# Scalars by a product with ones, masks behind the branch, and GpSimd set-up behind the first sink columns: the head of a fused attention and mixture-of-experts kernel

## The chip, the cores and the metric

The kernel runs on one core of one Trainium2 chip. The metric is the device time of one execution in microseconds. All times below that carry a place ("at 7.77") are counted from the start of the profiled span.

The engines are named as in the profile: PE is TensorE (PEld its weight loads), DVE is VectorE, ACT is ScalarE, POOL is GpSimd, SP is SyncE. A q behind a name is that engine's instruction queue, which issues DMAs and takes branches.

## The reference

Three layers follow each other. The first is attention over 4 batches, 8 heads, 768 positions and 64 columns, with a causal window and a few sink positions that every query sees:

```python
keep = is_sink | in_window          # pos < n_sink, 0 <= i - j < window
scores = np.where(keep, scale * q @ k.T, -1e9)
a = softmax(scores)                 # divided by sum + 1e-9
x = (a @ v) as [3072, 512]
x = np.maximum(x @ w_in, 0) ** 2 @ w_out          # 512 -> 2048 -> 512
```

The last layer is a mixture of eight experts. Each token takes the expert with the largest logit, and its result is scaled by the softmax weight of that expert and a sigmoid gate:

```python
out[mask] = gate_w * eom * (np.maximum(x[mask] @ w1[e], 0) @ w2[e])
```

`n_sink` (4) and `window` (128) are inputs, so the kernel reads them at run time.

## The kernel before

The kernel treats the 3072 tokens in 12 blocks of 256. For each block t, attention is done in four pairs of heads (p = 0 to 3) and two halves of 128 queries (n), then the block goes through the first feed-forward layer while the attention of the next block lies between its matrix products. The last part runs the experts over tokens that were sorted by expert.

The head is the time before the feed-forward layer of block 0 begins. It holds the constants, the attention of block 0, the start of block 1, and the first of the 32 pieces (512 KB each) of w_in and w_out, which must be rebuilt from raw bits: ScalarE does L310 and L313 on a piece, VectorE L317 and L318, and only then is its staging buffer free. The staging buffers (tag "stage") are a ring of three, handed out in the order in which the program asks for them; the ring also serves the scratch of `setup` and of `setup2`. The first three pieces have buffers of their own (`braw`) and are loaded from ScalarE's queue; all later ones come from SP's queue.

The steps of the head are events with places from -46 to 0 in a list. At each place h the program emits the events due, at -38 also `setup2`, and every third place one piece of the weights. A scheduler then orders the instructions of each engine by when it expects them to be ready and by priority, with events of the head ahead of others; what is wrapped in `pin` keeps its order among the pinned ones. Each engine works through its own list in order. So what the program says late may stand early in an engine's list, if it is ready, and one instruction that waits holds all behind it.

`scalars` loads n_sink and window into one partition (`one`, from SP and ScalarE), from which VectorE works out `gen`, the flag for a general path that is not taken here, and into all partitions (`raw`, two GpSimd loads with a stride of zero), which VectorE casts to `rawf` at L124. `setup` makes the identity and the masks: GpSimd fills `rel` and `col` with positions, and VectorE compares them with the scalars and writes M0, M1 and M2 (L214 to L219). Then a dozen idle products (`fill`, L101) keep TensorE working, and every engine loads `gen` and branches (L846, L847).

Behind the branch, for each pair of heads: `prep_k` transposes k on TensorE (L373), VectorE copies it into kT (L378), and GpSimd adds four columns per key block for the sinks (L380 to L384). `prep_q` does the same for q (L404, copy L411 or L409). `scores` multiplies (L461), VectorE adds the mask and finds the extremum (L469), ScalarE takes the exponential (L472), VectorE or ScalarE normalizes (L474 to L484). `ptrans` transposes P (L501, copied by ScalarE at L505), `pv` multiplies with v (L535). `prep_sink` readies the sink rows of v: GpSimd at L435 and L436, TensorE at L438. `setup2` makes all constants that later parts need, mostly on GpSimd; it zeroes the two `psk` tiles with VectorE casts (L263) from a zeroed scratch (L250), starts two stores, and loads the gate weights from SP, on which GpSimd then works (L258 to L261).

The first feed-forward products of block 0 are at L616 and read the rebuilt pieces with even numbers; those at L641 read the odd ones.

Of the kernel before, what the change touches and what calls it, by code (L numbers as in the profile page):

```python
# [46 lines left out]
def kern(ctx, tc, q, k, v, n_sink, window, w_in, w_out, w_gate, w_og, w1, w2, out):  # L47
# [49 lines left out]
    def fill(o, n):  # L97

        w = o.shape[-1]
        for _ in range(n):  # L100
            PE.matmul(o[:, 0:w // 128 * 128], lhsT=idle[:], rhs=idle[:, None, :].broadcast_to([128, w // 128, 128]), start=True, stop=True)  # L101


    def scalars(w):

        raw = w.tile([128, 2, 2], I32, name="raw")
        one = w.tile([1, 2, 2], I32, name="one")
        SY.dma_start(out=one[:, 0], in_=n_sink.bitcast(I32)[None, :])
        A.dma_start(out=one[:, 1], in_=window.bitcast(I32)[None, :])
        G.dma_start(out=raw[:, 0], in_=n_sink.bitcast(I32)[None, :].broadcast_to([128, 2]))  # L110
        G.dma_start(out=raw[:, 1], in_=window.bitcast(I32)[None, :].broadcast_to([128, 2]))
        c = w.tile([1, 3, 4], F32, name="c")
        for n, x in ((0, 0.0), (2, 1.0)):
            V.memset(c[:, 0, n:n + 1], x)
        for n, x in ((0, float(NS)), (2, 128.0)):
            V.memset(c[:, 1, n:n + 1], x)
        for n in range(2):
            V.memset(c[:, n, 1:4:2], 0.0)
        f = one[:].rearrange("p a w -> p (a w)")
        V.tensor_tensor(out=c[:, 2], in0=f, in1=c[:, 0], op=ALU.is_lt)  # L120
        V.tensor_tensor(out=c[:, 1], in0=f, in1=c[:, 1], op=ALU.is_gt)
        V.tensor_reduce(out=c[:, 0, 0:1], in_=c[:, 1:3], axis=AX.XY, op=ALU.max)
        V.tensor_copy(out=gen[:], in_=c[:, 0, 0:1])
        V.tensor_copy(out=rawf[:], in_=raw[:])  # L124
# [77 lines left out]
    def setup():  # L202
        make_identity(nc, ident)
        tmp = [cv.tile([128, 2 * XW], F32, tag="stage", bufs=3, name="tmp")]
        ns, wd = rawf[:, 0, 0:1], rawf[:, 1, 0:1]
        rel, col = tmp[0][:, 0:260], tmp[0][:, 260:388]
# [7 lines left out]
        V.tensor_scalar(out=M2[:], in0=rel, scalar1=wd, scalar2=NEG, op0=ALU.is_ge, op1=ALU.mult)  # L214
        V.tensor_scalar(out=col, in0=col, scalar1=ns, scalar2=NEG, op0=ALU.is_ge, op1=ALU.mult)
        V.tensor_tensor(out=M0[:], in0=M2[:, 132:260], in1=col, op=ALU.max)
        V.tensor_tensor(out=M1[:, 0:128], in0=M2[:, 0:128], in1=col, op=ALU.max)
        V.tensor_copy(out=M1[:, 128:260], in_=M2[:, 128:260])
        V.tensor_copy(out=M2[:, 128:132], in_=col[:, 0:NS])  # L219
        zz = tmp[0][:, 388:389]  # L220
        V.memset(zz, 0.0)
        A.activation(out=zz, in_=zz, func=AF.Exp)

    pin = tc.keep_in_program_order

    def setup2():

        G.memset(sel[:], 0.0)
# [4 lines left out]
        G.memset(blkm[:], 1.0)  # L233
        G.affine_select(out=blkm[:], in_=blkm[:], pattern=[[-16, 8]], compare_op=ALU.is_ge, fill=0.0, base=0, channel_multiplier=1)
        G.affine_select(out=blkm[:], in_=blkm[:], pattern=[[16, 8]], compare_op=ALU.is_ge, fill=0.0, base=15, channel_multiplier=-1)
        G.memset(ones[:], 1.0)
        G.affine_select(out=tri[:], in_=ones[:], pattern=[[1, 128]], compare_op=ALU.is_gt, fill=0.0, base=0, channel_multiplier=-1)
        G.iota(ek[:], [[-1, NE]], base=NE, channel_multiplier=0, allow_small_or_imprecise_dtypes=True)
        G.iota(eb[:], [[REG, NE]], base=0, channel_multiplier=0, allow_small_or_imprecise_dtypes=True)
        G.iota(tok[:], [[128, NT // 128]], base=0, channel_multiplier=1)  # L240
        G.memset(cum[:], 0.0)
        G.iota(sio[:], [[1, 32]], base=0, channel_multiplier=0, allow_small_or_imprecise_dtypes=True)
        G.memset(ltri[:], 1.0)
# [3 lines left out]
        G.memset(pf, NT)  # L247
        SY.dma_start(out=perm[:].rearrange("(p n) o -> p (n o)", p=128), in_=pf)
        zr = tmp[:, XW:2 * XW]
        G.memset(zr, 0.0)  # L250
# [5 lines left out]
        G.memset(w3[:], 0.0)  # L256
# [109 lines left out]
    def prep_k(t, p):  # L366
# [9 lines left out]
        if t < T32:  # L376
# [6 lines left out]
            for n in range(o, 2):  # L383
                G.tensor_copy(out=kf[:, n, 128:KS], in_=sk32[:, p])  # L384
# [487 lines left out]
    for h in range(-46, 0):  # L872
        run_to(h)
        if h == -38:
            setup2()
# [315 lines left out]
```

## Time and profile before

| what | value |
|---|---|
| three runs | 1149.51, 1151.32, 1152.0 us |
| median | 1151.32 us |
| profiled execution | 1149.8 us |
| its span, from the first to the last instruction | 1148.1 us |
| TensorE busy in it | 1120.3 us (98%) |
| VectorE, ScalarE, GpSimd busy | 727.9, 637.6, 417.0 us |
| mean granted TensorE clock | 0.995 |
| instructions | 23733 |

The profiled execution is one run that the hardware profiler recorded, and its span is 1.7 us shorter than its time. A busy TensorE is not TensorE at its peak, because products overlap and their ends are modelled. In the timelines, the bracket at the end of a row gives the idle time of the engine before it and what ended that idle time.

### The profile page before, as it was taken

How to read it: one execution, taken by the hardware profiler on the slowest of the kernel's cores; microseconds unless marked ns; L12 is line 12 of the kernel's file. 1: busy time of each engine (PE TensorE's matmuls, PEld its weight loads, DVE VectorE, ACT ScalarE, POOL GpSimd, SP SyncE). 2: the span in 40 equal slices, each digit the busy share in tenths (PEclk: the TensorE clock that was granted, in tenths of full speed). 3: DMA queues.
4: the chain of work that ended last, by engine and by line, in shares of the span. 5: the costliest groups of instructions: out<-in, count | busy, mean ns of one | idle time of the engine just before them, and what ended most of it. 6: DMA issues, size and time to landing. Idle time of an engine off the chain costs nothing. (4 is left out here: it accounts for less than half of the span.)

```text
span 1148.1 us, 23733 instructions
## 1 busy us (share of the span) xinstructions
PE 1120.3 (98%) x7002; PEld 941.3 (82%) x7002; DVE 727.9 (63%) x2027; ACT 637.6 (56%) x1749; POOL 417.0 (36%) x917
## 2 busy tenths in 40 slices
PE   7999999999999999999999999999999999999995
PEld 4556788888888888888888888997788888888884
DVE  4899877576766666676667676557412576764153
ACT  4898766777676767676767767454232232232200
POOL 3112563256564336565325655310211112221111
PEclk9999999999999999999999999999999999999998
DMA  6687111121211111211112110296411456653110
GB/s 154 179 234 211 39 24 46 39 54 34 54 29 50 38 45 38 56 28 44 36 38 56 38 31 1 28 253 162 129 39 47 155 185 218 220 206 134 48 45 24
DMA packets 139392, 100.08 MB, mean 87 GB/s; under 512 B 103908, under 2 KB 112228, under 8 KB 139239
## 3 DMA queue, kind: packets, MB, share of 16 engines
q1 hardware_dynamic: 131476, 82.28, 25.8%
q0 software_dynamic: 5472, 14.19, 3.7%
q10 hardware_dynamic: 2290, 1.84, 0.5%
q8 instruction: 64, 1.05, 0.4%
q14 instruction: 90, 0.73, 0.3%
HBM read 85.56 MB, written 13.76 MB: 87 GB/s over the span
## 5 line engine op out<-in xcount | busy, mean ns | idle before, releaser
L619 PE MATMUL psh<-xT,WI 128*128 128x256 f32 x2112 | 284.8, 285 | 0.0
L619 PEld LDWEIGHTS psh<-xT,WI 128*128 128x128 f32 x2112 | 270.6, 190 | 9.7 <-issue 0.4
L956 PE MATMUL psh<-WI,xt 128*128 (+1 forms) x672 | 162.1, 395 | 1.0 <-ACT xt L936 0.7
L629 DVE TENSOR_TENSOR r<-r 128x256 f32<-128x256 f32 x180 | 82.3, 458 | 116.8 <-ACT r L622 116.7
L644 PE MATMUL psx<-WOb,h 128*128 128x512 f32 x576 | 154.0, 404 | 0.8 <-ACT h L631 0.5
L956 PEld LDWEIGHTS psh<-WI,xt 128*128 128x128 f32 x672 | 123.8, 188 | 26.8 <-ACT xt L936 1.4
L644 PE MATMUL psx<-WOa,h 128*128 128x512 f32 x528 | 143.4, 406 | 0.0
L644 PEld LDWEIGHTS psx<-WOb,h 128*128 128x128 f32 x576 | 101.8, 188 | 19.9 <-ACT h L631 1.4
L472 ACT ACTIVATE P<-P,st 128x260 f32<-128x260 f32 (+1 forms) x192 | 93.8, 489 | 42.8 <-DVE st L469 42.7
L972 DVE TENSOR_TENSOR ht<-psht,ht 128x512 fp32r<-128x512 f32 x56 | 38.5, 689 | 120.7 <-ACT ht L936 120.3
L622 ACT ACTIVATE r<-psh 128x256 f32<-128x256 f32 x192 | 71.5, 372 | 66.1 <-PE psh L619 62.9
L644 PEld LDWEIGHTS psx<-WOa,h 128*128 128x128 f32 x528 | 92.7, 189 | 15.3
L517 POOL TENSOR_SCALAR_AFFINE_SELECT PT<-PT 128x256 fp32r<-128x256 f32 x224 | 98.4, 472 | 16.2 <-DVE PT L513 16.0
L994 POOL DMA_INDIRECT out_dram<-xg,pidx x28 | 28.7, 1024 | 198.8 <-ACT xg L993 158.0
L632 DVE TENSOR_TENSOR h<-r,h 128x256 fp32r<-128x256 f32 x184 | 83.8, 456 | 17.8 <-ACT h L631 12.0
L631 ACT ACTIVATE h<-r 128x256 fp32r<-128x256 f32 x184 | 76.1, 413 | 28.8 <-DVE r L629 24.4
L469 DVE CUSTOM_DVE_ANT_0 P<-pss,M 128x260 f32<-128x260 f32 (+1 forms) x184 | 72.7, 403 | 23.1 <-PE pss L465 11.3
L985 PE MATMUL psy<-WOb,ht 128*128 (+1 forms) x336 | 84.0, 398 | 0.0
L962 ACT ACTIVATE r<-psh 128x512 f32<-128x512 f32 x48 | 28.7, 598 | 98.6 <-PE psh L956 96.8
L985 PE MATMUL psy<-WOa,ht 128*128 (+1 forms) x336 | 82.2, 392 | 0.0
L484 ACT ACTIVATE P<-P,st 128x132 f32<-128x132 f32 (+2 forms) x168 | 62.2, 415 | 35.6 <-DVE st L475 35.4
L553 POOL TENSOR_TENSOR xr<-tB,tC 128x128 f32<-128x128 f32 x80 | 38.2, 478 | 103.1 <-DVE tB L552 98.3
(450 smaller groups left out, 1958.3 us busy)
## 6 DMA issues: line engine op xcount, KB each, us to landing
raw<-in_moe_w_dram SPq DMA_DIRECT2D x36, 1024.0 KB, 5.7
craw<-in_moe_w_out_dram SPq DMA_DIRECT2D x15, 512.0 KB, 4.0
craw<-in_moe_w_in_dram SPq DMA_DIRECT2D x14, 512.0 KB, 4.1
x2tab<-x2s SPq DMA_DIRECT2D x24, 256.5 KB, 3.1
kn<-in_k_dram SPq DMA_DIRECT2D x64, 96.0 KB, 2.2
vn<-in_v_dram SPq DMA_DIRECT2D x64, 96.0 KB, 2.2
qn<-in_q_dram SPq DMA_DIRECT2D x92, 64.0 KB, 2.1
kn<-in_k_dram SPq DMA_DIRECT2D x32, 64.0 KB, 2.0
```

Source lines behind the costliest of these rows:

```text
L469: V.tensor_tensor_reduce(out=P[:, e, 0:W], in0=ps[e][:, 0:W], in1=mask[:, 0:W], scale=-SCALE, scalar=3.0e38, op0=ALU.add, op1=ALU.min, acc ...
L472: A.activation(out=P[:, e, 0:W], in_=P[:, e, 0:W], func=AF.Exp, scale=-1.0, bias=st[:, e:e + 1], accum_out=st[:, 4 + e:5 + e])
L484: A.activation(out=P[:, e, 0:W], in_=P[:, e, 0:W], func=AF.Copy, scale=st[:, 6 + e:7 + e])
L517: G.affine_select(out=both[:, 1 - b, e], in_=bf[:, 0, e], pattern=[[0, 2], [1 - 2 * b, 128]], compare_op=ALU.is_gt if b else ALU.is_ge, fi ...
L619: PE.matmul(ps[:], lhsT=WI[:, j, a_, kk, :], rhs=x[:, b_, kk, :], start=(n == 0), stop=(n == 11))
L622: A.activation(out=hq[:], in_=ps[:], func=AF.Relu)
L629: E_.tensor_tensor(out=hq[:], in0=hq[:], in1=hq[:], op=ALU.mult)
L631: A.activation(out=o[:, 0], in_=hq[:], func=AF.Copy)
L632: V.tensor_tensor(out=o[:, 1], in0=hq[:], in1=o[:, 0].bitcast(F32), op=ALU.subtract)
L644: PE.matmul(acc[t][m][:], lhsT=o[:, a_, 128 * m:128 * m + 128], rhs=WO[j // 8][:, j % 8, b_, :], start=(j == 0 and n == 0), stop=(j == NF ...
L956: PE.matmul(ps[:], lhsT=o[:, a_, kk, :], rhs=wview(n, par + 2048 * b_ + 512 * kk, 512), start=(c == 0), stop=(c == 11))
L985: PE.matmul(yp[s][:], lhsT=o[:, a_, kk, :], rhs=wview(2 + n, par + 2048 * b_ + 512 * kk, 512), start=(n == 0 and kk == 0 and c == 0), stop ...
```

## The change

`scalars` no longer loads the scalars into all partitions. It copies the one row that it has into a row of a zeroed tile, and TensorE multiplies it with a tile of ones: every partition of the result holds the scalars, and VectorE casts it from PSUM into `rawf`. Three idle products of 256 columns stand ahead of that product, and six of 512 columns behind it in place of twelve. The scratch of `setup` is now requested in `scalars`.

`setup` keeps the GpSimd part of the masks. The VectorE part is the new function `masks`; its first half (M0, and M2 as it is) stands right behind the branch, its second half (M1, and the sink columns of M2) at place -42 of the list.

`setup2` moves from place -38 to -24. Its GpSimd instructions without an operand, and the first instruction of `prep_sink(0)`, are put behind the last sink column copy of pair 1 of block 0 on GpSimd by an ordering without a semaphore (`behind`).

```diff
-    def fill(o, n):
+    def fill(o, n, keep=False):
...
-        raw = w.tile([128, 2, 2], I32, name="raw")
         one = w.tile([1, 2, 2], I32, name="one")
         SY.dma_start(out=one[:, 0], in_=n_sink.bitcast(I32)[None, :])
         A.dma_start(out=one[:, 1], in_=window.bitcast(I32)[None, :])
-        G.dma_start(out=raw[:, 0], in_=n_sink.bitcast(I32)[None, :].broadcast_to([128, 2]))
-        G.dma_start(out=raw[:, 1], in_=window.bitcast(I32)[None, :].broadcast_to([128, 2]))
...
+        wide = w.tile([128, 2 * XW], F32, tag="stage", bufs=3, name="tmp")
+        full, row = wide[:, 512:640], wide[:, 640:644]
+        V.memset(full, 1.0)
+        V.memset(row, 0.0)
+        pb = psS.tile([128, 260], F32, tag="s1", name="psb")
+        fill(pb[:, 0:256], 3, True)
+        pin(V.tensor_copy(out=row[0:1], in_=f))
+        pin(PE.matmul(pb[:, 0:4], lhsT=full, rhs=row, start=True, stop=True))
         V.tensor_tensor(out=c[:, 2], in0=f, in1=c[:, 0], op=ALU.is_lt)
...
-        V.tensor_copy(out=rawf[:], in_=raw[:])
+        pin(V.tensor_copy(out=rawf[:].rearrange("p a w -> p (a w)"), in_=pb[:, 0:4]))
+        return wide
...
+    def masks(wide, n):
+
+        rel, col = wide[:, 0:260], wide[:, 260:388]
+        ns, wd = rawf[:, 0, 0:1], rawf[:, 1, 0:1]
+        if n == 0:
+            pin(V.tensor_scalar(out=M2[:], in0=rel, scalar1=wd, scalar2=NEG, op0=ALU.is_ge, op1=ALU.mult))
+            pin(V.tensor_scalar(out=col, in0=col, scalar1=ns, scalar2=NEG, op0=ALU.is_ge, op1=ALU.mult))
+            pin(V.tensor_tensor(out=M0[:], in0=M2[:, 132:260], in1=col, op=ALU.max))
+            return
+        pin(V.tensor_tensor(out=M1[:, 0:128], in0=M2[:, 0:128], in1=col, op=ALU.max))
+        pin(V.tensor_copy(out=M1[:, 128:260], in_=M2[:, 128:260]))
+        V.tensor_copy(out=M2[:, 128:132], in_=col[:, 0:NS])
...
     def setup2():
 
-        G.memset(sel[:], 0.0)
+        behind(G.memset(sel[:], 0.0))
...
+    skd = []
+
+    def behind(x):
+
+        tc.add_manual_dep(x.ins, skd[0].ins.name, mybir.DependencyInfo(mybir.DependencyClass.NoSync, mybir.DependencyReason.DATA),
+                          reason="order")
+        return x
...
             for n in range(o, 2):
-                G.tensor_copy(out=kf[:, n, 128:KS], in_=sk32[:, p])
+                x_ = G.tensor_copy(out=kf[:, n, 128:KS], in_=sk32[:, p])
+            if t == 0 and p == 1:
+                skd.append(x_)
...
-        G.tensor_copy(out=hl[0:32], in_=t[:])
+        x_ = G.tensor_copy(out=hl[0:32], in_=t[:])
+        if b == 0:
+            behind(x_)
...
-    scalars(cv)
+    wide = scalars(cv)
     for n in range(2):
         loads(0, n, "kq")
-    setup()
+    setup(wide)
     loads(0, 0, "v")
-    fill(psT.tile([128, 512], F32, tag="T", name="psi")[:], 12)
+    fill(psT.tile([128, 512], F32, tag="T", name="psi")[:], 6, True)
...
+    masks(wide, 0)
     loads(0, 1, "v")
...
-        if h == -38:
+        if h == -42:
+            masks(wide, 1)
+        if h == -24:
             setup2()
```

## Rows read from the trace of the kernel before

**Rows 1.** The page: the profiled execution's span.
```profile
span 1148.1 us, 23733 instructions
```

**Rows 2.** Busy time by stretch: stretch, PE, PEld, DVE, ACT, POOL, granted clock, DMA share, GB/s.
```profile
5.00:10.00 5.00, 2.50 (x17) 1.40 (x15) 1.85 (x8) 0.00 (x0) 1.20 (x7) 1.00 0.45 94
10.00:15.00 5.00, 1.78 (x10) 0.88 (x11) 2.12 (x11) 0.94 (x5) 4.05 (x23) 0.93 0.89 265
...
14.00:16.00 2.00, 2.00 (x9) 0.88 (x8) 1.32 (x7) 1.49 (x8) 0.19 (x2) 0.57 0.83 188
16.00:18.00 2.00, 2.00 (x13) 1.39 (x10) 0.72 (x4) 1.43 (x6) 0.00 (x0) 0.58 0.41 92
...
44.00:1148.00 1104.00, 1085.08 (x6802) 921.53 (x6802) 702.79 (x1917) 610.72 (x1669) 404.32 (x852) 1.00 0.30 84
```

**Rows 3.** Waits, 0 to 45: us in total, times, longest.
```profile
PE psx L461 <- POOL kT L384: 2.7, 1, 2.7
```

**Rows 4.** Timeline of DVE: start, us, engine, line, operation, tiles, count [idle before].
```profile
2.29 0.15 DVE L120 TENSOR_TENSOR c<-one,c 1x4 f32<-1x4 int32 x1 [1.12 <-DMA one<-in_n_sink_dram]
...
6.16 0.17 DVE L124 CAST rawf<-raw 128x4 f32<-128x4 int32 x1 [3.29 <-DMA raw<-in_window_dram]
...
7.81 0.35 DVE L214 TENSOR_SCALAR M<-tmp,rawf 128x260 f32<-128x260 f32 x1 [1.08 <-DVEq L847]
...
8.75 0.42 DVE L378 COPY kT<-psk__624 128x256 f32<-128x256 f32 x1
...
10.05 0.42 DVE L411 COPY qT<-psq 128x256 f32<-128x256 f32 x1 [0.81 <-PE psk__705 L373]
12.65 0.42 DVE L263 CAST psk<-tmp 128x128 fp32r<-128x128 f32 x2 [2.18 <-POOL tmp L250]
...
13.32 0.28 DVE L469 CUSTOM_DVE_ANT_0 P<-pss,M 128x128 f32<-128x128 f32 x1
...
39.67 0.69 DVE L318 SCALAR_TENSOR_TENSOR fw<-craw,fw 128x512 int32<-128x512 int32 x1
...
43.26 0.69 DVE L318 SCALAR_TENSOR_TENSOR fw<-craw,fw 128x512 int32<-128x512 int32 x1
```

**Rows 5.** Timeline of PE.
```profile
1.14 4.17 PE L101 MATMUL psi<-idle 128*128 128x512 bf16 x12 [1.14 <-DVE idle L95]
...
7.77 0.39 PE L101 MATMUL psk__624<-idle 128*128 128x512 bf16 x1 [2.13 <-DVEq L847]
...
41.04 0.33 PE L373 MATMUL psk__1106<-ident,kn 128*128 128x128 f32 x1 [0.87 <-ACT PT L505]
```

**Rows 6.** Timeline of ACT and its queue.
```profile
9.47 0.38 ACTq L298 DMA_DIRECT2D braw<-in_moe_w_in_dram  x1
9.88 0.52 ACTq L302 DMA_DIRECT2D braw<-in_moe_w_out_dram  x1
13.63 0.40 ACT L472 ACTIVATE P<-P,st 128x128 f32<-128x128 f32 x1 [8.79 <-DVE st L469]
...
17.36 0.38 ACT L505 ACTIVATE PT<-pspt 128x256 f32<-128x256 f32 x1 [0.57 <-PE pspt L501]
17.45 0.37 ACTq L298 DMA_DIRECT2D braw<-in_moe_w_in_dram  x1
```

**Rows 7.** Timeline of POOL: the first sink column operation.
```profile
12.57 0.18 POOL L380 CAST sk<-kT 128x4 fp32r<-128x4 f32 x1
```

**Rows 8.** Timeline of SP's queue.
```profile
30.47 1.01 SPq L354 DMA_DIRECT2D kn<-in_k_dram  x2
...
40.42 0.37 SPq L298 DMA_DIRECT2D craw<-in_moe_w_in_dram  x1
```

**Rows 9.** DMA issues at 1.7, 5.7 and 11.3: KB, us to landing.
```profile
kn<-in_k_dram SPq DMA_DIRECT2D x1, 64.0 KB, 3.1
...
vn<-in_v_dram SPq DMA_DIRECT2D x2, 64.0 KB, 3.6
...
qn<-in_q_dram SPq DMA_DIRECT2D x1, 64.0 KB, 5.4
```

More of the change, by code (lines that the diff above doesn't have):

```diff
@@ L95, in kern @@
     V.memset(idle[:], 1.0)
-    def fill(o, n):
+    pin = tc.keep_in_program_order
+    def fill(o, n, keep=False):
         w = o.shape[-1]
         for _ in range(n):
-            PE.matmul(o[:, 0:w // 128 * 128], lhsT=idle[:], rhs=idle[:, None, :].broadcast_to([128, w // 128, 128]), start=True, stop=True)
+            (pin if keep else lambda x: x)(PE.matmul(o[:, 0:w // 128 * 128], lhsT=idle[:], rhs=idle[:, None, :].broadcast_to([128, w // 128, 128]), start=True, stop=True))
     def scalars(w):
-        raw = w.tile([128, 2, 2], I32, name="raw")
         one = w.tile([1, 2, 2], I32, name="one")
@@ L200, in general, with setup @@
                 SY.dma_start(out=xtab[bass.ds(bh, 1), :, 128 * i:128 * i + 128].rearrange("o d s -> (o d) s"), in_=ot[:])
-    def setup():
+    def setup(wide):
         make_identity(nc, ident)
-        tmp = [cv.tile([128, 2 * XW], F32, tag="stage", bufs=3, name="tmp")]
-        ns, wd = rawf[:, 0, 0:1], rawf[:, 1, 0:1]
-        rel, col = tmp[0][:, 0:260], tmp[0][:, 260:388]
+        rel, col = wide[:, 0:260], wide[:, 260:388]
         G.iota(rel[:, 0:128], [[-1, 128]], base=128, channel_multiplier=1, allow_small_or_imprecise_dtypes=True)
@@ L213, in setup @@
         G.iota(col, [[1, 128]], base=0, channel_multiplier=0, allow_small_or_imprecise_dtypes=True)
[L214 to L220, printed above, removed]
+        zz = wide[:, 388:389]
         V.memset(zz, 0.0)
         A.activation(out=zz, in_=zz, func=AF.Exp)
-    pin = tc.keep_in_program_order
+    def masks(wide, n):
+        rel, col = wide[:, 0:260], wide[:, 260:388]
+        ns, wd = rawf[:, 0, 0:1], rawf[:, 1, 0:1]
[7 more added lines that the diff above has]
+        V.tensor_copy(out=M2[:, 128:132], in_=col[:, 0:NS])
     def setup2():
-        G.memset(sel[:], 0.0)
+        behind(G.memset(sel[:], 0.0))
         for n, r in ((0, 0), (4, 0), (8, 32)):
@@ L231, in setup2 @@
             G.affine_select(out=o, in_=o, pattern=[[-NS, 8], [-1, NS]], compare_op=ALU.not_equal, fill=1.0, base=0, channel_multiplier=1)
-        G.memset(blkm[:], 1.0)
+        behind(G.memset(blkm[:], 1.0))
         G.affine_select(out=blkm[:], in_=blkm[:], pattern=[[-16, 8]], compare_op=ALU.is_ge, fill=0.0, base=0, channel_multiplier=1)
         G.affine_select(out=blkm[:], in_=blkm[:], pattern=[[16, 8]], compare_op=ALU.is_ge, fill=0.0, base=15, channel_multiplier=-1)
-        G.memset(ones[:], 1.0)
+        behind(G.memset(ones[:], 1.0))
         G.affine_select(out=tri[:], in_=ones[:], pattern=[[1, 128]], compare_op=ALU.is_gt, fill=0.0, base=0, channel_multiplier=-1)
[L238 to L243, printed above, removed]
+        behind(G.iota(ek[:], [[-1, NE]], base=NE, channel_multiplier=0, allow_small_or_imprecise_dtypes=True))
+        behind(G.iota(eb[:], [[REG, NE]], base=0, channel_multiplier=0, allow_small_or_imprecise_dtypes=True))
+        behind(G.iota(tok[:], [[128, NT // 128]], base=0, channel_multiplier=1))
+        behind(G.memset(cum[:], 0.0))
+        behind(G.iota(sio[:], [[1, 32]], base=0, channel_multiplier=0, allow_small_or_imprecise_dtypes=True))
+        behind(G.memset(ltri[:], 1.0))
         G.affine_select(out=ltri[:], in_=ltri[:], pattern=[[1, NE], [-1, NE]], compare_op=ALU.is_ge, fill=0.0, base=0, channel_multiplier=0)
@@ L246, in setup2 @@
         pf = tmp[:, 0:NE * REG // 128].bitcast(I32)
-        G.memset(pf, NT)
+        behind(G.memset(pf, NT))
         SY.dma_start(out=perm[:].rearrange("(p n) o -> p (n o)", p=128), in_=pf)
         zr = tmp[:, XW:2 * XW]
-        G.memset(zr, 0.0)
+        behind(G.memset(zr, 0.0))
         SY.dma_start(out=x2tab[NT:NT + 1, :], in_=zr[0:1, :])
@@ L255, in setup2 @@
         pin(SY.dma_start(out=wg[0][:, :, NE:2 * NE], in_=w_og.rearrange("(k p) e -> p k e", p=128)))
-        G.memset(w3[:], 0.0)
+        behind(G.memset(w3[:], 0.0))
         part = [w3[:, :, 16 * n:16 * n + 16] for n in range(3)]
```

## The prediction

> **What bounds the kernel now.** I read the page first for its span [rows 1], then busy time by stretch [rows 2]. From 44 us to the end TensorE is busy for 1085.08 of 1104.00 us. Whatever the head saves therefore has to be a shift: TensorE's dense work begins earlier and the rest follows. Before that, TensorE has work for only half of 5 to 10 us (2.50 of 5.00) and a third of 10 to 15 us (1.78 of 5.00), and in 14 to 16 us its granted clock is 0.57, near the lower of its two levels (1.2 of 2.4 GHz), after that sparse stretch. So the room is in the first 18 us.
>
> The list of waits of the head [rows 3] has TensorE waiting 2.7 us for the sink columns that GpSimd writes into kT. The timelines by engine [rows 4 to 7] give the order. The scalars are in one partition early, since VectorE works on `one` at 2.29. But the cast of `raw`, and so the masks and the branch behind it, stand until 6.16, after 3.29 of waiting for the window load that GpSimd issued; VectorE's next mask comes at 7.81, after 1.08 of branch. TensorE's first fill behind the branch is released by VectorE's branch at 7.77, after 2.13 idle. The copy of kT is made at 8.75, but the first score sum (L469) comes 4.57 later, at 13.32, because two casts of psk (L263) stand ahead of it and wait for a memset of the set-up. GpSimd's sink columns (L380) come at 12.57 behind the same set-up. ScalarE's first exponential is at 13.63, after 8.79 of waiting for VectorE's sum, its first copy of transposed P at 17.36.
>
> **Scalars.** Removed: two GpSimd loads. Added: two memsets, a row copy, four columns of product, a cast from PSUM. The memsets fall into VectorE's wait for `one` (the idle time before L120 is 1.12), so they cost nothing; without that cover they would cost some 0.2 each, the size of the 0.17 cast. Row copy 0.17, from 2.29 on: 2.5. The trace has no product this short. Its cost lies between 0 and the 0.39 of a 512-column fill [rows 5]; I take 0.4, since latency rather than columns sets it, and 0.2 for the two hand-overs. Cast 0.17: rawf is there at 3.2 to 3.3 in place of 6.33 [rows 4]. The 1.08 of branch stays, so VectorE's first mask comes at 4.4 in place of 7.81. The pinned masks are three operations of about the 0.35 of L214 or less, done by 5.4, before a kT can be copied; the two of M1 that now stand behind the branch are the same work in a place where VectorE waits for TensorE.
>
> **TensorE behind the branch.** Its start is the latest of three. VectorE's branch: 4.4. The second k load, issued at about 1.7: it takes 3.1 to land, 4.8 [rows 9]. Its own fills: twelve took 4.17 from 1.14 [rows 5], 0.35 each; now three of half the width, a wait for the row copy until 2.5, the product of 0.4, six more at 0.35, 2.1: 5.0, and 0.2 for the hand-over. So 5.2 in place of 7.77, a gain of 2.5 (bounds 2.0, if the six fills and the transposes all run slowly, and 2.9, the k load). The kT copy moves from 8.75 to 6.2.
>
> The Trainium skill (TensorE: Matmul & The Clock Gate, Part 1) holds that the array is throttled by default, is released by activity, and falls back after idle time; that speaks against fewer fills with a hole among them. The 0.57 of 14 to 16 us, behind the sparse stretch, agrees [rows 2]. By the rule I would expect the first transposes at half pace, by estimate 0.4 more, and a result of 1148.5; by the rows alone, 1148.1.
>
> **Set-up behind the sink columns.** The queue in front of VectorE's first score sum loses the wait of 2.18 for L263 [rows 4]. It keeps the q copy, which starts 1.3 behind kT (10.05 less 8.75, in the trace because of the next k transposes) and takes 0.42, and the scores, about 0.6: 6.2 + 2.4 = 8.6 in place of 13.32. GpSimd writes the sink columns right behind the kT copy, at 6.7 in place of 12.57 [rows 7], so TensorE's wait of 2.7 goes.
>
> **What is late next is ScalarE.** Its queue holds two 512 KB loads, at 9.47 and 9.88, the second 0.52 long: it is free at 10.40 [rows 6]. They follow the landing of the last v load (issued at 5.7, 3.6 long: 9.3) [rows 9], and the change touches neither; less traffic may give some tenths. So the first exponential comes at 10.4, not at 8.7: a gain of 3.2 there, not 4.7. From it to the copy of transposed P were 3.73, part of it waiting for VectorE's late sums and for slow TensorE work (0.57 in the row of the copy). Now four score tiles are ready when ScalarE starts: I take 2.9, so 13.3 for 17.36, a gain of 4.0. Bounds: 3.2, if nothing is caught up, and 5.0, if the lower clock of 14 to 18 us goes (4 us at 0.57 to 0.58 would take 2.3 at full clock, of which ScalarE lets through about a half [rows 2]). The dense work carries it on.
>
> **What the change costs later.** The set-up's staging buffer was the second of the ring of three and becomes the fifth, between the loads of weight pieces 5 and 6 (counted from 0). Piece 6 must then wait for the end of piece 4 (43.26 + 0.69) instead of piece 3 (39.67 + 0.69) [rows 4], on whose end its load now starts (40.42) [rows 8]: 3.6 later. Bounds 0 and 3.6; I take 0.5, since ScalarE and VectorE have other pieces' splits to do, and TensorE reads piece 6 only in the fourth of the first products. The two casts of psk (0.42 for both) leave an idle VectorE for a busy one: 0 to 0.4, I take 0.3. The masks' other parts, the moved GpSimd operations and the stores of perm and x2tab lie beside work on other engines; uncovered, the GpSimd part would cost the 2 to 3 us that it costs today.
>
> **Sum.** 4.0 - 0.5 - 0.3 = 3.2 us. The profiled execution has 1148.1 of span and 1.7 around it, 1149.8; 1146.6 after. The median of the three runs is 1151.32, 1.5 above it; I predict the median: 1148.1. 0.2% is 2.3 us, about what can be told from no change here.
>
> **Rivals.**
> *ScalarE's queue holds.* The third 512 KB load is issued by ScalarE itself, at 17.45, between its copies [rows 6]. If its turn (as with loads on SP, which are seen to wait for earlier landings) depends on the q load of p = 2, issued at 11.3 and 5.4 long [rows 9], ScalarE cannot pass it before 16.7. Everything else comes 4 us earlier and then stands there: 17.45 - 16.7 = 0.75 is all that is left, 1150.6. For it: that load's landing is bound by 1 MB of weights ahead of it, and no edit moves them. Against it: the order of the queue is laid out anew, and the load may slip behind other work. Chance 0.23.
>
> *SP stands at the gate loads (slower).* The set-up's loads into its staging buffer now need the end of piece 3: 40.36, or 36.4 when shifted by 4.0. If they stand on SP ahead of the k loads of t = 1 that were issued at 30.47 [rows 8], those are issued at about 37 and land at 40.1 with the 3.1 above, where their transposes (41.04) would be due at 37.0 [rows 5]. That eats 3.1 of the 4.0, and the q, v and piece loads behind them, some 3 us of issue more, push the next stage by about as much again: 3 us slower, 1154. It decides as soon as the gate loads precede that one pair of k loads. Against it: SP's issue order follows when buffers are expected to be free. Chance 0.15.
>
> *More than the sum.* The sparse stretch goes, TensorE stays at its upper level, and the staging delay is hidden: 5.5, so 1145.8. Chance 0.12.
>
> *The forecast:* 0.50, its own range 1146.8 to 1149.4.
>
> Faster by over 0.2%: 0.45 of the forecast and 0.12, 0.57. Within: 0.05 and 0.23 and 0.02 of the slower rival, 0.30. Slower: 0.13. The range reaches over the larger gain, the forecast and the held queue, and leaves the slower rival out: 1145.2 to 1152.0.
>
> **What would show it.** Right: in the timeline after, rawf near 3.3, TensorE's first k transposes before 6, L469 near 8.6 with no wait for L250, sink columns right behind the kT copy, the first exponential at the end of ScalarE's two load issues near 10.4, the first copy of transposed P near 13.3, first products (L616) some 3.5 earlier than before. Wrong: an exponential far behind 10.4 or a hole in ScalarE ending with its third load (first rival), an SP queue idle before the gate loads with TensorE waiting for k (second), or the 4.0 present at 20 us and gone at 60 us, which would be the staging ring.

## The result, and the profile after

The changed kernel takes 1157.63 us (median of 6 runs, 1157.07 to 1161.32) where the kernel before takes 1151.54 in the runs beside it: a ratio of 1.0061, 95% interval 1.0047 to 1.0076 (ratios here are estimated from all executions of both kernels, so they need not be the quotient of the two medians). It is slower by 6.1 us, outside the range that was given. The profiled execution of it has 1157.69, with a span of 1156.0 for 1148.1 [rows 1].

The head begins as forecast. These are VectorE's timeline, then GpSimd's and TensorE's, of the changed kernel: start, length, engine, line, operation, tiles, [idle before]. The lines are those of the changed kernel: its L396 is L378 of before, L491 is L469, L398 is L380.

```profile
3.15 0.16 DVE L131 COPY rawf<-psb 128x4 f32<-128x4 f32 x1 [0.19 <-PE psb L126]
4.60 0.36 DVE L228 TENSOR_SCALAR M<-tmp,rawf 128x260 f32<-128x260 f32 x1 [1.29 <-DVEq L869]
...
7.32 0.42 DVE L396 COPY kT<-psk__620 128x256 f32<-128x256 f32 x1 [1.85 <-PE psk__620 L391]
...
8.84 0.29 DVE L491 CUSTOM_DVE_ANT_0 P<-pss,M 128x128 f32<-128x128 f32 x1
```
```profile
7.81 0.19 POOL L398 CAST sk<-kT 128x4 fp32r<-128x4 f32 x1 [5.57 <-DVE kT L396]
```
```profile
5.84 0.58 PE L103 MATMUL psk__620<-idle 128*128 128x512 bf16 x1
6.22 0.63 PE L103 MATMUL psq<-idle 128*128 128x512 bf16 x1
...
17.00 0.69 PE L523 MATMUL pspt<-ident,P 128*128 128x128 f32 x2 [6.44 <-ACT P L506]
```

The scalars are cast at 3.15 for 6.16, the first score sum stands at 8.84 for 13.32 with no wait for the set-up, the sink columns come at 7.81 for 12.57 [rows 4, 7]. Then everything stops: TensorE is idle for 6.44 us before the first transposes of P, waiting for ScalarE. ScalarE's timeline with its queue says for what:

```profile
14.11 0.45 ACTq L316 DMA_DIRECT2D braw<-in_moe_w_in_dram  x1
14.60 0.53 ACTq L320 DMA_DIRECT2D braw<-in_moe_w_out_dram  x1
15.17 0.40 ACT L494 ACTIVATE P<-P,st 128x128 f32<-128x128 f32 x1 [10.30 <-issue]
...
17.72 0.38 ACT L527 ACTIVATE PT<-pspt 128x256 f32<-128x256 f32 x1
...
21.17 0.37 ACTq L316 DMA_DIRECT2D braw<-in_moe_w_in_dram  x1
21.59 0.28 ACT L560 ACTIVATE xT<-psh 128x128 f32<-128x128 f32 x1 [3.09 <-DMA qn<-in_q_dram]
21.96 0.60 ACT L527 ACTIVATE PT<-pspt 128x512 f32<-128x512 f32 x1
```

Its two 512 KB loads go at 14.11 and 14.60, not at 9.47 and 9.88 [rows 6], and the first exponential comes behind them at 15.17. The sums it needs were there at 8.84 to 9.99. At the first copy of transposed P the changed kernel is still only 0.36 behind (17.72 for 17.36 [rows 6]); at the second it is 2.0 behind, 21.96 for this one of the kernel before:

```profile
19.93 0.60 ACT L505 ACTIVATE PT<-pspt 128x512 f32<-128x512 f32 x1
```

SyncE's queue, then the list of waits of that queue for 5 to 16 us, then the instructions of its branch line (count, lengths in ns, first and last start), show what held ScalarE's two loads:

```profile
8.18 0.39 SPq L320 DMA_DIRECT2D craw<-in_moe_w_out_dram  x1
8.62 0.42 SPq L316 DMA_DIRECT2D craw<-in_moe_w_in_dram  x1
14.09 0.89 SPq L372 DMA_DIRECT2D kn<-in_k_dram  x2
```
```profile
SPq L869 <- SPq L869: 4.3, 1, 4.3
```
```profile
L869 SPq EVENT_SEMAPHORE  x8: 17/17/17, 13.4 to 14.0; - x8
L869 SPq COMPARE_BRANCH  x1: 50/50/50, 9.1 to 9.1; - x1
```

Two loads of weight pieces (craw, pieces 3 and 4 counted from 0, 512 KB each) are issued at 8.18 and 8.62, ahead of SyncE's branch (L869). The branch itself takes 50 ns at 9.1. Behind it the program has SyncE pass eight semaphore instructions, which wait for loads issued on its queue: the first of them comes at 13.4, and the trace records the last landing of the second piece at 13.40. SyncE's next load goes at 14.09 (10.29 before for the same k load, L354 there), and ScalarE's loads at the same moment; the view of L869 names ScalarE's first exponential as what waited for SyncE there, 10.3 us long. Below, "SyncE's branch" means the branch with these waits.

In the kernel before, neither of these pieces is among SyncE's issues up to 18.6; piece 3 goes at 19.63, right behind the two stores and the two gate loads of the set-up:

```profile
10.29 0.90 SPq L354 DMA_DIRECT2D kn<-in_k_dram  x2
...
19.63 0.50 SPq L302 DMA_DIRECT2D craw<-in_moe_w_out_dram  x1
```

The line of DMA traffic of the changed kernel for 6 to 16 us, in 40 slices of 0.25 us and tenths of the 16 engines, has the two pieces arrive until about 12.75, and then nothing until the queues go on:

```profile
DMA  0541010361019654999899999930000000002854
```

The busy time by stretch (columns as in [rows 2]) shows the price on TensorE's side: nearly nothing done in 10 to 15 us, and then 10 us at a granted clock of 0.50 to 0.60 of 2.4 GHz, near its lower level (the last row is of the kernel before).

```profile
10.00:15.00 5.00, 0.56 (x7) 0.26 (x4) 0.15 (x3) 0.00 (x0) 2.91 (x17) 0.88 0.52 187
15.00:20.00 5.00, 2.93 (x10) 1.29 (x10) 1.82 (x10) 3.32 (x12) 0.00 (x0) 0.50 0.93 282
20.00:25.00 5.00, 5.00 (x20) 2.42 (x19) 1.03 (x6) 2.24 (x8) 0.00 (x0) 0.60 0.79 213
```
```profile
20.00:25.00 5.00, 5.00 (x36) 2.97 (x37) 3.18 (x15) 3.93 (x13) 1.12 (x7) 1.00 0.78 230
```

In 20 to 25 us TensorE is busy throughout in both kernels, but does 20 products in the changed one and 36 before, at 1.00.

What happens later is read from three groups of TensorE's products: those of the first feed-forward layer in all token blocks but the first (xT, WI, 256 columns), those of the first block (xT, fw), and one of the two halves of the second products of the experts (psy, 512 columns). The columns are the count, the lengths in ns (least, median, greatest), and the start of the first and of the last of the group in us. First before, then after:

```profile
L619 PE MATMUL psh<-xT,WI x2112: 274/283/385, 125.5 to 780.4; 128*128 128x256 f32 x192
L616 PE MATMUL psh<-xT,fw x128: 377/379/483, 43.9 to 121.7; 128*128 128x256 f32 x128
...
L985 PE MATMUL psy<-WOa,ht x336: 387/389/477, 802.0 to 1133.0; 128*128 x156, 128*128 128x512 f32 x12
```
```profile
L641 PE MATMUL psh<-xT,WI x2112: 274/280/388, 129.1 to 782.6; 128*128 128x256 f32 x192
L638 PE MATMUL psh<-xT,fw x128: 377/379/483, 47.2 to 127.9; 128*128 128x256 f32 x128
...
L1010 PE MATMUL psy<-WOa,ht x336: 388/396/483, 804.3 to 1141.1; 128*128 x156, 128*128 128x512 f32 x12
```

The head leaves the changed kernel 3.3 us late (47.2 for 43.9), and 3.6 at 125.5. So most of the head's loss arises behind the first copy of transposed P, where the clock is low and the loads of the next pairs, which SyncE issues behind its branch, come 3.8 us later; no run separates these two. The first layer then takes 653.5 us from first to last start where it took 654.9, with a median of 280 ns for 283, so it wins 1.4 back. The expert group takes 336.8 for 331.0, with 396 ns for 389: 5.8 lost. Nothing that the change edits works in these 1000 us. Two causes, then: SyncE's branch in the head, and something that changes the pace of products everywhere.

For the second, the positions of the tiles in SBUF are a candidate. The change removes the tile `raw`, and with it a slot of 32 bytes at the upper end, so the tiles of attention (att), of the first layer (xT, h, moe) and of the experts (xt, ht, m3) all start 32 bytes higher. By the layout of the pools that is at offset 0 of 256 bytes instead of 224; no trace holds addresses, so only the shift of 32 bytes is certain. (The constant HOME, 224, in the code sets that offset for the weights at the lower end.)

### The profile page after: what moved, and what is told of

Read it like the earlier page. It is cut to its first block, busy times and chain, and to the rows that moved or that the text cites. A ratio compares the mean times of both kernels' runs of the same rounds, so it can differ in the third digit from the quotient of the medians.

```text
span 1156.0 us, 23732 instructions
## 1 busy us (share of the span) xinstructions
PE 1123.8 (97%) x7001; PEld 936.1 (81%) x7001; DVE 727.1 (63%) x2030; ACT 637.1 (55%) x1749; POOL 421.0 (36%) x915
## 5 line engine op out<-in xcount | busy, mean ns | idle before, releaser
L641 PE MATMUL psh<-xT,WI 128*128 128x256 f32 x2112 | 280.7, 282 | 1.3 <-DVE xT L605 0.7
L641 PEld LDWEIGHTS psh<-xT,WI 128*128 128x128 f32 x2112 | 266.9, 188 | 12.2 <-DVE xT L605 0.9
L981 PE MATMUL psh<-WI,xt 128*128 (+1 forms) x672 | 165.0, 399 | 1.6 <-ACT ht L961 0.9
L1019 POOL DMA_INDIRECT out_dram<-xg,pidx x28 | 31.4, 1121 | 201.5 <-ACT xg L1018 160.0
L491 DVE CUSTOM_DVE_ANT_0 P<-pss,M 128x260 f32<-128x260 f32 (+1 forms) x184 | 72.2, 402 | 17.3 <-PE pss L487 7.7
```

Source lines behind the costliest of these rows:

```text
L491: V.tensor_tensor_reduce(out=P[:, e, 0:W], in0=ps[e][:, 0:W], in1=mask[:, 0:W], scale=-SCALE, scalar=3.0e38, op0=ALU.add, op1=ALU.min, acc ...
L641: PE.matmul(ps[:], lhsT=WI[:, j, a_, kk, :], rhs=x[:, b_, kk, :], start=(n == 0), stop=(n == 11))
L981: PE.matmul(ps[:], lhsT=o[:, a_, kk, :], rhs=wview(n, par + 2048 * b_ + 512 * kk, 512), start=(c == 0), stop=(c == 11))
```

## The experiments

Times are medians; the kernel before ran beside each, at 1151.0 to 1151.4. The ratio to it stands with its interval.

**e1_pad** gives the changed kernel its old positions back.

```diff
     def scalars(w):
 
+        w.tile([128, 2, 2], I32, name="raw")
         one = w.tile([1, 2, 2], I32, name="one")
```

> The changed kernel with one tile of 16 bytes per partition left allocated but unused where raw stood, so that all later SBUF tiles lie where they lay before the change. Theory 1 (two causes: a late head and shifted operand addresses): the products of the experts run at their old pace again (median start to start 227 ns instead of 233), the 5.5 us lost after 800 us go, the 2.1 us gained between 130 and 760 us go as well; what the head lost, 4.3 us at 130 us, stays: about 1155.8 us. Theory 2 (all of the loss is a consequence of the head's order): no change, 1157.6 us. First exponential at 15.2 us under both.

Measured: 1155.08, ratio 1.0030 (1.0019 to 1.0040).

**e2_addr** takes the same 32 bytes from the kernel before, and nothing else.

```diff
-        raw = w.tile([128, 2, 2], I32, name="raw")
+        raw = sk32[:, 0].bitcast(I32).rearrange("p (a w) -> p a w", a=2)
...
-        V.tensor_copy(out=rawf[:], in_=raw[:])
+        V.tensor_copy(out=rawf[:], in_=raw)
```

> The kernel before, with raw placed inside the tile sk32 instead of a tile of its own: the order of work stays, all later SBUF tiles lie 32 bytes lower in the ring of 256 as in the changed kernel. Theory 1 (addresses set the pace of the products): minus 2.1 us between 130 and 760 us, plus 5.5 us in the experts, so about 1154.9 us, with 233 ns per product of 512 columns in the experts. Theory 2: 1151.5 us and 227 ns.

Measured: 1154.12, ratio 1.0033 (1.0020 to 1.0045). The two groups of e1_pad, then of e2_addr:

```profile
L642 PE MATMUL psh<-xT,WI x2112: 274/283/386, 130.0 to 785.7; 128*128 128x256 f32 x192
...
L1011 PE MATMUL psy<-WOa,ht x336: 387/389/477, 807.3 to 1138.5; 128*128 x156, 128*128 128x512 f32 x12
```
```profile
L619 PE MATMUL psh<-xT,WI x2112: 274/280/387, 125.8 to 779.3; 128*128 128x256 f32 x192
...
L985 PE MATMUL psy<-WOa,ht x336: 388/396/483, 801.0 to 1137.2; 128*128 x156, 128*128 128x512 f32 x12
```

With the padding the changed kernel has 283 and 389 ns again, and 331.2 us for the experts. Without the tile the kernel before has 280 and 396, and 336.2. So 32 bytes of position, with no work changed, cost 2.6 to 2.8 us by the medians (by the stages of the profiled executions of e2_addr and of before, 5.2 lost less 1.4 won, 3.8), and e1_pad's remaining 3.7 us are not of position. They are the head's, to which its profiled execution adds a granted clock of 0.69 in 45 to 50 us, where the changed kernel has 1.00.

**e3_behind** adds one edit to e1_pad: the loads of pieces 3 and 4 keep their place in the program order, behind the branch.

```diff
-        if c < NBOOT:
+        if c < NBOOT + 2:
             tc.keep_in_program_order(x)
```

> As e1_pad, with the two loads of weight pieces 3 and 4 pinned, so that SP issues them behind its branch and not ahead of it. Theory 1 (SP's way past the branch waits for every load that it has issued, and ScalarE's two piece loads wait for SP): SP is past its branch near 9.3 us, first exponential near 10.4 instead of 15.2, and the forecast's gain of 3.2 us appears: about 1148.3 us. Rival (ScalarE's queue is then held by its third piece load until the q load of p = 1 has landed): first exponential at 10.4, but a hole in ScalarE up to about 16.5, and 1150.6 us.

Measured: 1148.33, ratio 0.9982 (0.9973 to 0.9991), 6.8 under e1_pad; 4.0 of it are there at the first products of block 0 (42.9; e1_pad 46.9). ScalarE's timeline, then the stretches:

```profile
9.77 0.46 ACTq L317 DMA_DIRECT2D braw<-in_moe_w_in_dram  x1
...
10.84 0.40 ACT L495 ACTIVATE P<-P,st 128x128 f32<-128x128 f32 x1 [5.96 <-POOL ones L247]
...
13.39 0.38 ACT L528 ACTIVATE PT<-pspt 128x256 f32<-128x256 f32 x1
...
16.96 0.38 ACTq L317 DMA_DIRECT2D braw<-in_moe_w_in_dram  x1
17.38 0.28 ACT L561 ACTIVATE xT<-psh 128x128 f32<-128x128 f32 x1 [3.20 <-DMA qn<-in_q_dram]
```
```profile
10.00:15.00 5.00, 2.29 (x10) 1.19 (x9) 1.88 (x10) 3.32 (x12) 2.90 (x17) 0.77 0.79 250
15.00:20.00 5.00, 5.00 (x21) 2.54 (x20) 0.95 (x5) 2.13 (x8) 0.00 (x0) 0.55 0.74 188
```

The loads go at 9.77 and 10.26, the first exponential at 10.84, the first copy of transposed P at 13.39. This is the head of the forecast, and the theory that SyncE's branch held ScalarE's loads stands. But ScalarE then stands 3.20 us, until its third piece load can go at 16.96 behind the landing of a q load: the first rival's hole. And the first transposes, P V products and second scores run between 12.7 and 19 us at the lower level (granted clock 0.53 in 12.5 to 15 us, 0.50 in 15 to 17.5), after TensorE stood still for 2.64.

**e14_move** asks what let the loads forward. It is the kernel before with the set-up called later, and nothing else of the change.

```diff
-        if h == -38:
+        if h == -24:
             setup2()
```

> The kernel before with one edit: the set-up of the routing tables is called at h = -24 instead of -38, nothing else of the change (addresses as before). SyncE's order then has pieces 3 and 4 ahead of its branch, as in the changed kernel. The theory that this move, by the staging ring, is what let the loads forward and that SyncE's branch waits for their landing: SyncE passes its branch at 12.5 to 13.5 us instead of about 9, ScalarE's two loads go at 13.5 to 14.7 instead of 9.47 and 9.88, the first exponentials at 15, and the time is 1155.5 (1153.5 to 1157). The rival, that the loads forward cost nothing by themselves (the sum of the head is bound by the sink columns at 13.3 anyway): 1150.5 to 1152.

Measured: 1152.60, ratio 1.0017 (1.0008 to 1.0026). SyncE's timeline and its waits:

```profile
7.32 0.39 SPq L302 DMA_DIRECT2D craw<-in_moe_w_out_dram  x1
7.76 0.43 SPq L298 DMA_DIRECT2D craw<-in_moe_w_in_dram  x1
13.52 0.73 SPq L361 DMA_DIRECT2D vs<-in_v_dram  x1
```
```profile
SPq L847 <- SPq L847: 4.6, 1, 4.6
```

The mechanism is there in full: both loads ahead of the branch, 4.6 us in it, ScalarE's loads at 13.53 and 13.94 and the first exponential at 14.51. The first copy of transposed P comes at 17.07, even 0.3 before that of the kernel before, and still the first products of block 0 start at 46.9 for 43.9, after a granted clock of 0.50 in 15 to 20 and 0.59 in 20 to 25 us: here too the loss lies behind that copy. The time lies between the ranges of the theory (1153.5 to 1157) and of the rival (1150.5 to 1152). The price is 1.6 us by the medians against 3.4 by the spans of the profiled executions (1151.5 and 1148.1); this execution lies 0.6 above the median of its own runs, that of before 1.5 under the median of its.

**e9_front** is the converse: e1_pad with the set-up back in its old place.

```diff
-        if h == -24:
+        if h == -38:
             setup2()
...
     def behind(x):
-        tc.add_manual_dep(x.ins, skd[0].ins.name, ...)
         return x
```

> As e1_pad (the changed kernel with the old addresses), but GpSimd's set-up stands where it stood in the kernel before, ahead of the sink columns: the product with ones and the masks behind the branch are left of the change. The theory that the set-up's buffer being second in the staging ring was what kept the two piece loads behind SyncE's branch: SyncE passes its branch at about 9 us with no 4 us wait, ScalarE's two loads go at 9.8 and 10.3 and the first exponentials at 10.9 as in e3_behind, but the sink columns come at about 13.4, so that the 260-column score sums lose 2 to 3 us against e3_behind: 1150 (1149 to 1151.5), 4 to 6 us under e1_pad. The rival, that the moved branch and masks alone already delay ScalarE's loads: first exponential at 15 and 1154 to 1156, as e1_pad.

Measured: 1151.80, ratio 1.0003 (0.9994 to 1.0012). The loads stay behind the branch, ScalarE's go at 9.66 and 10.07, and its first exponential comes at 10.64. So the place of the set-up is what kept the pieces back. That it did so by its buffer, the second of the ring, is not shown: piece 3 had a free buffer in the kernel before too, the third of the ring, and went behind the set-up's stores and loads on SyncE all the same (19.63; here 20.19). The buffer and the place in SyncE's queue moved together. The cost is where it was put, but larger: the sink columns come at 13.37 to 14.62, so that the 260-column sum waits until

```profile
15.59 0.43 DVE L490 CUSTOM_DVE_ANT_0 P<-psx,M 128x260 f32<-128x260 f32 x1 [7.08 <-PE psx L482]
```

So the moved set-up is worth 3.5 us (1151.80 less 1148.33) once the two loads are kept behind, and without it the rest of the change is worth nothing that can be measured.

Two experiments aim at ScalarE's hole in e3_behind. **e4_sp** issues the third piece load from SyncE, **e5_late** later in the program (it goes at 21.23 there, for 16.96).

```diff
-            raw, dq = braw[c], A
+            raw, dq = braw[c], A if c < 2 else SY      # e4_sp
```
```diff
-    fetch(NBOOT)
+    fetch(2)                                           # e5_late
```

> As e3_behind, with the third piece load issued by SP instead of ScalarE. If ScalarE's third load is what holds the head, ScalarE has no hole before 17 us and the time is 1 to 3 us below e3_behind; if the head is held by landings of q and k, it equals e3_behind within 0.5 us.

> As e3_behind, but ScalarE's third piece load is issued only three steps later, behind its first widening activation. The theory that the 3.2 us hole of ScalarE at 14.2 (that load standing behind the q loads in the queue) gives back most of what the earlier start won: no ScalarE idle stretch over 1 us between 11 and 18 us, the shift against the kernel before stays at -3.5 to -4.5 us at 15 to 25 us instead of falling to -1.1, and the time is 1145.5 (1144.5 to 1146.5), 2 to 3 us under e3_behind. The rival, that the hole is covered (the half granted clock at 15 to 20 us or the order of the later pieces sets the pace there): the hole is gone, but the shift at 25 us is -1.1 again, 1148.3; and if the later landing of the third piece delays the feed-forward of block 0, as in e4_sp, 1150 to 1151.

Measured: e4_sp 1151.17, ratio 0.9999 (0.9991 to 1.0008); e5_late 1149.97, ratio 0.9984 (0.9975 to 0.9992). Both take the hole away, and neither is faster than e3_behind. In e4_sp the piece's 512 KB land ahead of the next pair's loads: the second pair of k loads goes at 18.03 instead of 15.08. In e5_late TensorE is busy throughout at a granted clock that is low there too,

```profile
15.00:20.00 5.00, 5.00 (x20) 2.31 (x20) 1.37 (x8) 3.45 (x10) 0.00 (x0) 0.65 0.48 109
```

and the second copy of transposed P comes at 17.75 for 17.94, the third at 22.59 for 22.78. In the head the hole was covered: taking it away wins 0.2 in e5_late. What both lose to e3_behind lies further on, in part at least in the clock: e5_late, whose first products of block 0 start at 42.5, has a granted clock of 0.74 in 40 to 45 us, and e4_sp (43.2) 0.73 in 110 to 116 and 0.66 in 140 to 145, where e3_behind has 1.00. So the theory that the hole gives back most of the gain finds no support; e4_sp's time lies in neither of the ranges expected of it.

**e12_some** and **e11_warm** then aim at the clock, with idle products ahead of the first transposes of P: two of 256 columns, or three of 512.

```diff
             fill(ps[:].rearrange("p n c -> p (n c)"), 2)
+            for _ in range(2 if p + n == 0 else 0):
+                PE.matmul(ps[...][:, 0:256], lhsT=ident[:], rhs=ident[:, None, :].broadcast_to([128, 2, 128]), ...)
```

> As e3_behind with two idle float32 products of 256 columns (0.85 us together) ahead of the first transposes of P; the order of every other engine stays. TensorE's standstill before the first transposes falls from 2.6 to about 1.8 us. The theory of the lower clock: if the clock does not fall after the shorter standstill, the shift at 25 us is -2.5 to -3.5 and the time 1146.5; if it falls all the same, it falls later or for as long, and the time is 1147.8 to 1148.5. The rival (loads and ScalarE's queue set the pace): -1.4 and 1148.3 whatever the clock does.

> As e3_behind, with three idle float32 products of 512 columns (0.85 us each at the upper clock by the 0.11 us of a 128-column transposing product with two passes in hand, about 2.6 us together) ahead of the first transposes of P, in the 2.6 us in which TensorE stands still before 12.67. The scheduler orders ScalarE's and SyncE's work somewhat otherwise from about 13 us on. The theory that the head's gain is lost because the first transposes, P V products and second scores run at the lower clock from 12.7 to 19 us (in the kernel before six idle products lie in that stretch instead): granted clock 0.95 or more in 10 to 15 and 15 to 20 us, the shift at 25 us -2.5 to -3.5 instead of -1.4, time 1146.5 (1145.5 to 1147.5). The rival, that the loads and ScalarE's queue set the pace there: the clock is up and the shift at 25 us is -1.4 again, 1148.3; the changed order can add up to 1.5 us at 45 to 140 us to either.

Measured: e12_some 1147.81, ratio 0.9969 (0.9958 to 0.9980); e11_warm 1155.75, ratio 1.0041 (1.0027 to 1.0055). Of e12_some the stretches, and the place in TensorE's timeline where its lead ends:

```profile
15.00:20.00 5.00, 4.28 (x29) 2.35 (x28) 2.20 (x10) 2.96 (x12) 0.07 (x1) 1.00 0.72 189
20.00:25.00 5.00, 3.99 (x22) 1.93 (x20) 1.91 (x11) 3.40 (x11) 0.53 (x4) 1.00 0.58 129
```
```profile
12.53 0.33 PE L526 MATMUL pspt<-ident,P 128*128 128x128 f32 x1 [2.43 <-ACT P L507]
...
21.36 0.30 PE L425 MATMUL psq<-ident,qn 128*128 128x128 f32 x1 [1.01 <-DMA qn<-in_q_dram]
```

The standstill is 2.43 instead of 2.64 (1.8 was expected), and the granted clock stays at 1.00. The length of the standstill does not decide that alone: e4_sp has one of 2.42 and then 0.50 in 15 to 20 us. The 260-column scores come 1.9 earlier than in e3_behind (15.67 for 17.53), but the third copy of transposed P only 0.4 (22.35): TensorE waits 1.01, until 21.36, for a q load. So with the clock up the loads of the next pair are the limit; the time is 0.5 under e3_behind, with overlapping intervals, and 1.3 above what the clock theory gave. No run takes ScalarE's hole, the low clock and the late loads away together. e11_warm missed: the clock is up (1.00 in 10 to 15, 0.78 in 15 to 20 us), but in the other order of the engines the third piece load stands ahead of the first copy of transposed P, ScalarE waits 4.00 there, and TensorE stands still for 3.05 after it. Its time is 2.5 above its profiled execution, which has a mean granted clock of 0.995; its four other executions have 0.992.

Two experiments put the phases at different positions. **e8_home** was to do so with a tile in the experts' own pool, **e10_two** does it with a pool of its own; both are e3_behind without e1_pad's padding.

```diff
-        w.tile([128, 2, 2], I32, name="raw")
...
+    m3p = ctx.enter_context(tc.tile_pool(name="m3p", bufs=1, side="right"))    # e10_two
+    m3p.tile([128, 8], F32, name="gap2")
     m3 = ctx.enter_context(tc.tile_pool(name="m3", bufs=2, side="right"))
+    m3.tile([128, 8], F32, name="gap2", bufs=1)                                # e8_home
```

> As e3_behind, but the padding of 32 bytes stands in the expert phase's own pool alone: xT, h2 and the attention tiles have the addresses of the changed kernel (offset 0 in 256 bytes), xt and ht of the expert phase those of the kernel before (offset 224). The theory that each phase's matmul pitch hangs on where its own operands stand: 256-column products of the first layer at 120.0 ns, 512-column products of the expert phase at 227, so about 2 us less than e3_behind in the first 800 us and nothing lost behind it: 1146.2 (1145.3 to 1147.2). The rival, that the pitch of the expert phase follows something earlier (the padding as such, the order of instructions): 233 ns there and 1151.5 to 1152.5; and if the first layer's gain was not one of position, 1148.3.

> As e8_home, but the 32 bytes now lie above the expert phase's tiles (a pool of their own, opened ahead of theirs), so that xt, r2 and ht of the expert phase do start at offset 224 of 256 bytes, and xT, h2 and the attention tiles at 0. The theory that each phase's matmul pitch hangs on where its own stationary and moving tiles stand: 120.0 ns for the 256-column products of the first layer, 227 for the 512-column products of the expert phase, the shift against e3_behind -1.2 at 800 us and no loss behind it: 1147.0 (1145.8 to 1148). The rival, that the expert phase's pitch follows the weights or anything else that moved: 233 ns and 1151 to 1152.5, as e8_home.

Measured: e8_home 1151.98, ratio 1.0002 (0.9993 to 1.0011); e10_two 1145.53, ratio 0.9955 (0.9941 to 0.9969). In e8_home the padding came to lie below the experts' tiles instead of above them, so xt and ht still start at offset 0: it is the changed kernel with only the two loads held back, 5.65 under it. Its time and its slow pace in the experts (396 ns) are what its rival gave; that the padding missed its place is read from the layout and borne out only by the next run. In e10_two they start at 224, and xT and h at 0 (by the same layout):

```profile
L641 PE MATMUL psh<-xT,WI x2112: 274/280/387, 122.8 to 776.1; 128*128 128x256 f32 x192
L638 PE MATMUL psh<-xT,fw x128: 377/379/483, 42.5 to 121.7; 128*128 128x256 f32 x128
...
L1010 PE MATMUL psy<-WOa,ht x336: 387/389/481, 797.8 to 1128.9; 128*128 x156, 128*128 128x512 f32 x12
```

Both phases now have their faster pace, 280 and 389 ns: 653.3 us for the first layer, 331.1 for the experts. **e13_both** adds e12_some's products to it.

> e10_two and e12_some together. If the two are independent, e12_some's 0.5 to 1.5 us (the granted clock at 1.00 from 10 to 25 us) come on top of e10_two: 1144.5 (1143.5 to 1145.3), shift at 800 us about -5 against the kernel before. If what e12_some won at the head is lost again (ScalarE's hold by the third piece load and the q load of the next pair set the pace), 1145.5 as e10_two.

Measured: 1145.21, ratio 0.9953 (0.9939 to 0.9967). The granted clock is 1.00 from 10 to 25 us and the first products of block 0 come at 42.0 instead of 42.5, but the time can't be told from e10_two's. Either of them is faster than both kernels, by 5.8 us than the kernel before and by 12 than the changed one.

## Why the prediction was wrong

**The step that failed** is ScalarE's: "They follow the landing of the last v load [...], and the change touches neither." The change does touch it. With the set-up moved behind pieces 3 and 4, the scheduler puts their loads ahead of SyncE's branch. SyncE stands there until they have landed (its waits end at 14.0, in the kernel before at 9.3), and ScalarE's two loads go only with SyncE's next one. The first exponential came at 15.17 instead of 10.4, the first copy of transposed P at 17.72 instead of 13.3, and the loads of the next pair 3.8 us later than before, where the sum had none of this. e3_behind (6.8 us back for one line), e14_move (the move alone brings the loads forward) and e9_front (without the move they stay) show it from three sides. The prediction followed the move only to where it delays a piece (piece 6, 3.6 later at most, by the ring) and never asked which loads it lets go earlier, or what stands behind them on SyncE. Whether the ring or the set-up's place in SyncE's queue had held them is open.

**What was not in the sum** is position. Nobody reads 5.8 us in the experts out of a change to the head, but a removed tile is in the diff, and the code names an offset. e1_pad, e2_addr and e10_two show it: 2.6 us of the 6.1 by the medians (1157.63 less 1155.08).

**The rest by its steps.** The scalars: rawf at 3.15 (3.2 to 3.3), first mask 4.60 (4.4); the short product took 0.59, not 0.4. TensorE behind the branch: 5.84 for 5.2, since its own fills ended at 5.69 and not at 5.0: the six took 2.72, 0.45 each, and the 0.35 of the prediction was a mean of twelve, taken over both levels of the clock. The kT copy: 7.32 for 6.2; the two fills in front of it took 0.58 and 0.63 and started 0.38 apart, where those of e3_behind took 0.38 each, started 0.21 apart, and the copy stands at 6.79. The pace fits the clock: the trace's first record of a granted clock, of 1.00, begins at 6.93 us in the changed kernel, at 5.83 in e3_behind and at 4.03 in the kernel before, and the 1.00 that the view of stretches prints ahead of it is no record. The Trainium skill's rule (TensorE: Matmul & The Clock Gate, Part 1), that the array is throttled until activity releases it, had the prediction put 0.4 more on this place. The changed kernel agrees, with 0.53 between the two copies of kT. Sink columns: right behind the kT copy, 7.81 (6.7). Score sum: 8.84 (8.6), close by luck, since the kT copy came 1.1 later than forecast and the q copy straight behind it (7.66), not 1.3 after its start. First copy of transposed P: 17.72, and 13.39 in e3_behind (13.3), so the gain of 4.0 at that place was right once ScalarE's loads are free. "The dense work carries it on" was wrong: of 4.0 at 13.4 us there are 1.0 left at the first products of block 0, which start at 42.9 in e3_behind for 43.9 before. TensorE's chain there runs at the lower level after its standstill; in the kernel before, idle products lie in that slow stretch. With the clock up (e12_some) ScalarE's hold and the next pairs' loads take over. That these three cover each other is argued, not shown: the hole and the low clock were each taken away alone, and neither gave the gain back. The costs named for later (0.5 and 0.3) were isolated by no run.

That e3_behind comes out at 1148.33, with 1148.1 forecast, is therefore partly luck. By the spans of the profiled executions (1146.8 and 1148.1) its head wins 1.3, by the medians 3.0. The profiled execution of before is 1.5 under its median and that of e3_behind 0.2 above. The mean granted clock tells them apart: of the executions of before beside the experiments, 21 have 0.995, as the profiled one, with a median of 1150.2, and 38 have 0.992, with 1151.8. How much of the 4.0 really arrives lies between 1.3 and 3.0.

**The rivals.** The first is right in its mechanism, a ScalarE hole that ends with the third load (3.09 in the changed kernel, 3.20 in e3_behind), and its price is not confirmed: without the hole neither e4_sp nor e5_late is faster than e3_behind. The second named SyncE and the right side, but other loads, at 30 instead of 8 us. The third did not come.

## What to carry to other kernels

When a part of the program with buffers and loads of its own is moved, list the loads that may now go earlier, not only those that must go later, and look what stands behind them in the same queue: where the program waits at a branch for the loads issued ahead of it, an early load that seems free becomes a stall of all that follows. Before timing a change that adds or removes a tile, compare the start addresses of all later tiles; a difference there is a change of its own, to be run alone. And a gain at one place of a sparse head is worth only what the next limits let through: here the clock after a standstill, ScalarE's queue and the loads of the next pair stood behind it, and taking away one of the first two gave little.

## What the hardware showed

- Products with the same shapes and the same work run at another pace when their tiles start 32 bytes elsewhere: 512-column products of the experts 389 ns at the old positions and 396 at those 32 bytes higher, 256-column products of the first layer 283 and 280 (median lengths, all at a granted clock of 1.00; before, changed kernel, e1_pad, e2_addr and e10_two). The two go in opposite directions, so neither position is best for both. Which of the operands does it was not separated.
- SyncE's branch that is not taken took 50 ns. What held the queue at it for 4.3 us (e14_move 4.6) were waits that this program holds there for loads issued on that queue, two of 512 KB just ahead of it; in the kernel before, where the last loads ahead of it are v loads of 64 KB or less, they took 1.9 in five parts.
- After a standstill of 2.64 us TensorE's granted clock was 0.55 in 15 to 20 us (e3_behind), after one of 2.42 it was 0.50 (e4_sp); with two more idle products of 256 columns ahead and a standstill of 2.43 it stayed at 1.00 (e12_some).
- Executions of one program differ in their mean granted clock, and in time with it: the kernel before has a median of 1150.2 us at 0.995 and of 1151.8 at 0.992.
